# Two casts to a slot on ScalarE, the head's exponential behind them, and the DMAs that move along

## The chip, the cores and the metric

The kernel runs on one core of a Trainium2 chip. It has five instruction streams: TensorE (PE, matmuls; PEld is its weight load), VectorE (DVE), ScalarE (ACT), GpSimd (POOL) and SyncE (SP), which issues nearly all DMAs here. [...] The metric is the device time of one execution in microseconds, with the median of several runs. All inputs are float32, one sequence of 2048 tokens with width 512.

## What is computed

Four residual layers, of two kinds in turn (A, B, A, B). With 32 heads of width 16:

```python
def _A_ref(x, wqkv, w_phi, wo):      # linear attention over softmax features
    ...
    phi_q = jnp.concatenate([_softmax(pq, axis=-1), _softmax(-pq, axis=-1)], axis=-1)
    ...
def _B_ref(x, wq, wk, wv, wo, beta): # N = 4 segments of L = 512 tokens
    phi = lambda t: jnp.where(t > 0, t + 1.0, jnp.exp(t))
    ...
    for s in range(N):
        qs, ks, vs = q[:, :, s], k[:, :, s], v[:, :, s]
        logits = jnp.einsum("bhqd,bhkd->bhqk", qs, ks) * scale + mask
        p = _softmax(logits, axis=-1)
        a_dot = jnp.einsum("bhqk,bhkd->bhqd", p, vs)
        pq = phi(qs)
        num = jnp.einsum("bhld,bhde->bhle", pq, M)
        den = jnp.einsum("bhld,bhd->bhl", pq, z)[..., None] + 1e-6
        o = g * (num / den) + (1.0 - g) * a_dot
        pk = phi(ks)
        M = M + jnp.einsum("bhld,bhle->bhde", pk, vs)
        z = z + jnp.einsum("bhld->bhd", pk)
    ...
x = x + _A_ref(_layernorm(x), ...); x = x + _B_ref(_layernorm(x), ...)
x = x + _A_ref(_layernorm(x), ...); x = x + _B_ref(_layernorm(x), ...)
```

The change concerns the two B layers alone: causal softmax attention inside a segment of 512 tokens, plus a memory M, z that is read and written from segment to segment.

## The kernel before

**Half chunks and slots.** A B layer is one long hand-written order (`LayerB.steps`). Each of its 4 segments has 8 half chunks of 4 heads each, which I call h0 to h7. A half chunk is cut into R = 5 slots; the first is its *head* (slot 0), and slots 1 to 4 follow. In each slot `attend` puts score matmuls of the half chunk into the PSUM tile `lg`, of which there is one (`PS("lg", 1, ...)`), and ACT takes the exponential into `P`. So the `lg` matmuls of a slot wait for the exponential of the slot before. POOL zeroes the masked part of `P` (affine_select). Beside them `maxima` computes score maxima for a later half chunk (matmuls into `mx`, `my` or two `g` tiles, reduced by DVE into `mxs`), and the rest of a slot is filled with six steps of some projection.

**The head.** Slot 0 also does what a half chunk does once: transposes (`hh`, `oh`, `KN` and `mxs` rows: a matmul with `ident` into a `g` tile, which ACT then copies or casts out), memory reads and writes, and `weighted`, the 32 matmuls of `P` by `v` for the half chunk before. There are four `g` tiles (G = 4), so the matmuls of `weighted` wait until ACT has emptied a `g` tile of the head; ACT then moves their result into `U`.

**Projections in pairs.** `mm3_pair` runs two projections together on the two row halves of PE, in 24 steps, six in each of slots 1 to 4. The halves change places twice, before step 6 (the first of slot 2) and before step 18 (the first of slot 4). At each change PE waits for an empty instruction (`sync.nop`) on SP, which in turn waits for the matmuls of the step before. I call these two the first and the second handoff. They stand in SP's stream among its DMAs. Six steps of a pair are called Q (queries and keys of a chunk), V (values) or O (output projection) in the tables: h0 and h1 have Q2 and Q3, h2 and h3 O, h4 Q0 of the next segment, h5 V, h6 Q1, h7 V. In the last segment of a layer h2 to h5 have O (second B layer), or h2, h3 O and h4, h5 V of the next layer (first B layer).

**What follows a pair.** After a Q pair, at the end of slot 4, ACT copies the two results to `raw` (tiles `tb`), one for queries (m = 0) and one for keys (m = 1). `projected` then gives three jobs for each, which run some slots later (`self.at`): `parts` casts to `ta` (the high part; POOL subtracts the low part), `features` computes relu and exponential, `added` sums them on POOL. After an O pair ACT copies two results to `tb`, POOL adds them to the residual rows (`xr` or `mmq`), and SP stores these.

**Stacks.** `stack` has SP copy the high and low parts into the score operands (`e<-ta`, three DMAs for the queries, side 0, and three for the keys, side 1). It is called in the slots named by STACK for the half chunk three further on; the maxima of the next head read what it brings. A stack waits for `parts` where these were only just computed, which is so in h1, h5 and h7.

**Order.** Instructions of one engine keep the order in which the program names them (`Ordered`, `held`). In a slot this order is: scores and exponential, maxima, postponed jobs (`at`), stacks, the "<" entries of the table (head work), `weighted`, rows of the norm ("n", which run one slot after their entry), and last the six steps of the pair.

Of the kernel before, what the change touches and what calls it, by code (L numbers as in the profile page):

```python
# [10 lines left out]
AF = mybir.ActivationFunctionType  # L11
ALU = mybir.AluOpType
# [6 lines left out]
P = 128  # L19
NSEG = 4  # L20
# [12 lines left out]
G = 4  # L33
R = 5
TB3 = 5
STACK = (1, 3)
SPARE = (2, 4)
XR = 2
FILL = (1, 3, 4)
# [25 lines left out]
7.0 <max <a0+ | 7.1 fin V+/6 w      | 7.2 V+/6 n        | 7.3 V+/6 n | 7.4 V+/6 w  # L65
"""
GAPS = """
0.0 <max <a0 | 0.1 fin Q2/6 n       | 0.2 Q2/6 n        | 0.3 Q2/6 n cv3 | 0.4 Q2/6
1.0 <t0 <turn <max <a1 m0 | 1.1 fin Q3/6 | 1.2 Q3/6 n   | 1.3 Q3/6 | 1.4 Q3/6
2.0 <ln <t1 <turn <max <a1 m1 | 2.1 fin O/6 | 2.2 O/6   | 2.3 O/6 | 2.4 O/6  # L70
3.0 <ln <turn <turn <max <a2 | 3.1 fin O/6 | 3.2 O/6    | 3.3 O/6 | 3.4 O/6
4.0 <ln <ln <max <a2 | 4.1 fin Q0+/6 | 4.2 Q0+/6 cv0    | 4.3 Q0+/6 cv1 | 4.4 load begin Q0+/6
# [2 lines left out]
7.0 <max <a0+ | 7.1 fin V+/6      | 7.2 V+/6 n N        | 7.3 V+/6 n N | 7.4 V+/6  # L75
"""
LAST = """
0.0 <max <a0 | 0.1 fin Q2/6 n       | 0.2 Q2/6 n        | 0.3 Q2/6 n cv3 | 0.4 Q2/6
1.0 <turn <max <a1 | 1.1 fin Q3/6   | 1.2 Q3/6 n        | 1.3 Q3/6 | 1.4 Q3/6
2.0 <ln <turn <max <a1 | 2.1 fin O/6 | 2.2 O/6          | 2.3 O/6 | 2.4 O/6  # L80
3.0 <ln <turn <turn <max <a2 | 3.1 fin O/6 | 3.2 O/6    | 3.3 O/6 | 3.4 O/6
4.0 <ln <ln <max <a2 | 4.1 fin v/2  | 4.2 v/2 cv0       | 4.3 v/2 cv1 | 4.4 v/2
# [19 lines left out]
def interleave_kernel(ctx, tc, x_in, a_wqkv, a_wphi, a_wo, b_wq, b_wk, b_wv, b_wo, b_beta,  # L102
                      c_ident, c_mask, c_bd, out):
    nc = tc.nc
    MUL, ADD, SUB, MAX, MIN = ALU.mult, ALU.add, ALU.subtract, ALU.max, ALU.min
# [14 lines left out]
    def T2(tag, bufs, dt=F32, shape=(P, 512)):  # L120
        return sp.tile(list(shape), dt, tag=tag, bufs=bufs, name=nm(tag))

    def PS(tag, bufs, shape=(P, 512)):
        return ps.tile(list(shape), F32, tag=tag, bufs=bufs, name=nm(tag))
# [38 lines left out]
    dve, act, pool, sync = [Ordered(e) for e in (nc.vector, nc.scalar, nc.gpsimd, nc.sync)]  # L163
# [19 lines left out]
    def dma(out, in_):  # L183
        sync.dma_start(out=out.bitcast(F32), in_=in_.bitcast(F32))
# [319 lines left out]
    def out_pair(tiles, xdst, w, soon, w0=0, w1=D):  # L504

        pos = [PS("g", G) for _ in tiles]

        def side(po, o):
            return po[:, 0 : w1 - w0], o, lambda b, kc: w[b][:, kc, w0:w1]

        yield from mm3_pair(*[side(po, o) for po, (x, i, o) in zip(pos, tiles)])
        for po, (x, i, o) in zip(pos, tiles):
            y = T2("tb3", TB3)[:, 0 : w1 - w0]
            act.copy(y, po[:, 0 : w1 - w0])
            pool.tensor_tensor(out=x[:, w0:w1], in0=y, in1=x[:, w0:w1], op=ADD)
            if w1 == D:
                soon(lambda x=x, i=i: sync.dma_start(out=xdst[i], in_=x))
        yield

    def weigh(out, p, eps, add, eng=pool):  # L520
# [460 lines left out]
    class LayerB:  # L981
# [53 lines left out]
        def proj_pair(self, s, c):  # L1035

            self.st.setdefault((s, c), {})
            hT, ws = self.hT[s], self.w4
            pps = [PS("g", G) for _ in range(2)]

            def side(pp, w):
                return pp, lambda a, kc: w[:, a, kc, :], lambda b, kc: hT[b][:, kc, :]

            for n, _ in enumerate(mm3_pair(*[side(pp, w) for pp, w in zip(pps, ws)])):
                if n == 12:
                    for m in range(2):
                        self.queue_w(m, (0,))
                yield
            jobs = []
            for m in range(2):  # L1050
                self.queue_w(m, (1,))
                jobs.append(self.projected(s, c, m, pps[m]))
            for m, job in enumerate(jobs):
                for n, f in zip((1, 2, 3) if m == 0 else (2, 4, 5), job):
                    self.at.setdefault(self.k + n, []).append(f)
            yield

        def projected(self, s, c, m, pp):

            d = self.st[s, c]  # L1060
            hi, lo = d["part", m] = [T2("ta1", TA, F32R) for _ in range(2)]
            raw = T2("tb3", TB3)
            act.copy(raw, pp)

            def parts():
                act.copy(hi, raw)
                (pool if self.k >= R else dve).tensor_tensor(out=lo, in0=raw, in1=hi.bitcast(F32), op=SUB)
            todo = [parts]
            if not (s == 0 if m == 0 else s == NSEG - 1):
                e = d["phi", m] = T2("tb2", TB2)  # L1070

                def features():
                    act.activation(e, raw, AF.Relu, scale=-1.0)
                    act.activation(e, e, AF.Exp, scale=-1.0)
                    if m == 1:
                        act.activation(raw, raw, AF.Relu)

                def added():
                    if m == 0:
                        pool.tensor_scalar(raw, raw, 0.0, None, op0=MAX)  # L1080
                    pool.tensor_tensor(out=e, in0=raw, in1=e, op=ADD)
                todo += [features, added]
            return todo

        def sums(self, s, c):
# [107 lines left out]
        def attend(self, m):  # L1193


            s, c, hf = m // 8, m % 8 // 2, m % 2
            Q, K = [t[:, 2 * hf : 2 * hf + 2, :] for t in self.st[s, c]["set"]]
            self.pr[m] = {}

            def prod(pb, r, kb, at, w):  # L1200
                for e in range(2):
                    q, k = Q[64 * e : 64 * e + 64, r, :], K[64 * e : 64 * e + 64, r, :]
                    mm(pb[e][:, at : at + w], lhsT=k[:, kb * P : (kb + 1) * P],
                       rhs=q[:, 512 - w : 512], start=True, stop=True, tile_position=(64 * e, 0))

            for kbs, r in (((0,), 0), ((0,), 1), ((1, 3), 0), ((1, 3), 1), ((2,), None)):
                apart = self.thin and self.k > 8 * R * NSEG - 9 and self.k % 2
                if apart:
                    pb = [PS(t, 1) for t in ("mx", "my")]
                else:  # L1210
                    both = PS("lg", 1, (P, 2, 512))
                    pb = [both[:, e] for e in range(2)]
                pr = T2("P4", NP4, shape=(P, 2, 512))
                pq = pr.rearrange("p e (b x) -> p e b x", b=4)
                if kbs == (0,):
                    prod(pb, r, 0, 0, 512)
                    diags = [pr[:, :, 0:P]]
                elif kbs == (1, 3):
                    prod(pb, r, 3, 256, 256)
                    prod(pb, r, 1, 0, 384)  # L1220
                    diags = [pq[:, e, 0:4:3, :] for e in range(2)]
                else:
                    for rr in range(2):
                        prod(pb, rr, 2, 256 * rr, 256)
                    diags = [pr.rearrange("p e (r x) -> p (e r) x", r=2)[:, :, 0:P]]
                self.pr[m][kbs, r] = pr
                with tc.high_priority():
                    for out, src in ([(pr[:, e], pb[e]) for e in range(2)] if apart else [(pr, both)]):
                        act.activation(out, src, AF.Exp, scale=0.25)
                for diag in diags:  # L1230
                    pool.affine_select(out=diag, in_=diag, pattern=[[0, diag.shape[1]], [1, P]],
                                            compare_op=ALU.is_ge, fill=0.0, base=0, channel_multiplier=-1)
                yield

        def weighted(self, m):
# [75 lines left out]
        def out(self, s):  # L1311
            layer, i = (self.layer, NT - 4) if s < 0 else (self, 4 * s)
            for t in (0, 2):
                tiles = [(x, i + t + n, oT) for n, (oT, x) in enumerate(self.turned[0:2])]
                del self.turned[0:2]
                parts = 2 if self.thin and s == NSEG - 2 else 1
                for n in range(parts):
                    yield from out_pair(tiles, layer.xdst, layer.wo, lambda f: self.at.setdefault(self.k + (5 if s < NSEG - 2 else 2), []).append(f),
                                        n * D // parts, (n + 1) * D // parts)

        def early(self):
# [59 lines left out]
        def steps(self, side, after, table_end):  # L1381
# [3 lines left out]
            N = 8 * NSEG  # L1385
# [76 lines left out]
            for s in range(NSEG):  # L1462
                for cell in (FIRST if s == 0 else GAPS if s < NSEG - 1 else table_end).replace("|", "\n").split("\n"):
                    if cell.strip():
                        at_, *what = cell.split()
                        m, j = at_.split(".")
# [3 lines left out]
            for k in range(BEGIN, R * N + 1):  # L1470
                self.k = k
                if 0 <= k < R * N:
                    next(at)
                if MAXIMA <= k < MAXIMA + 2 * R or 2 * R - LEAD <= k < R * N - LEAD:
                    next(ma)
                put_off[0] = None
# [5 lines left out]
                m = k // R + 3  # L1482
                if 2 <= m < N:
                    for side_ in range(2):
                        if k % R == STACK[side_]:
                            self.stack(m, side_)
                what, s = table.get(k, ((), 0))
                for w in what:
                    if w[0] == "<":
                        do(w[1:], s, k)  # L1490
                if k % R == 0 and 0 <= k // R - 1 < N:
                    self.weighted(k // R - 1)
                for f in self.rows:
# [91 lines left out]
```

## Time and profile before

| | |
|---|---|
| median of 3 runs | 1368.67 us (1368.21 to 1370.08) |
| the profiled execution | 1368.75 us, span 1367.0 us |
| PE busy | 1290.1 us, 94% of the span |
| ACT busy | 840.8 us, 62% |
| DVE, POOL busy | 1038.3 us (76%), 752.6 us (55%) |
| chain that ended last | PE 62%, DVE 14%, ACT 13%, issue 4%, POOL 3%, DMA 3% |

The B layers lie at about 285 to 697 us and 953 to 1365 us of the span. A row of the waits names the waiting engine and tile, what it waited for, the sum in us, the number of waits and the longest. A row of the timeline gives the start, the duration, engine, line, operation, output and inputs, the count of instructions merged into the row, and in brackets the idle time before it with the one that ended it. SPq rows are DMA issues on SP; their duration is that of the issue, not of the transfer.

### The profile page before, as it was taken

How to read it: one execution, taken by the hardware profiler on the slowest of the kernel's cores; microseconds unless marked ns; L12 is line 12 of the kernel's file. 1: busy time of each engine (PE TensorE's matmuls, PEld its weight loads, DVE VectorE, ACT ScalarE, POOL GpSimd, SP SyncE). 2: the span in 40 equal slices, each digit the busy share in tenths (PEclk: the TensorE clock that was granted, in tenths of full speed). 3: DMA queues.
4: the chain of work that ended last, by engine and by line, in shares of the span. 5: the costliest groups of instructions: out<-in, count | busy, mean ns of one | idle time of the engine just before them, and what ended most of it. 6: DMA issues, size and time to landing. Idle time of an engine off the chain costs nothing.

```text
span 1367.0 us, 41870 instructions
## 1 busy us (share of the span) xinstructions
PE 1290.1 (94%) x16552; PEld 989.6 (72%) x16552; DVE 1038.3 (76%) x3247; ACT 840.8 (62%) x1274; POOL 752.6 (55%) x1116
## 2 busy tenths in 40 slices
PE   7999989999999999999899998999999999999987
PEld 6887868776766766777668886786776777677665
DVE  4766778787887887887757767787788788787884
ACT  5556345547787677676644334454677767767754
POOL 1568666225557667666334446551456566666653
PEclk9999999999999999999999999999999999999999
DMA  5398437544554444546341103745455454444432
GB/s 204 101 338 272 147 126 233 175 110 131 173 163 138 138 129 122 146 131 170 103 155 63 63 32 125 231 150 165 137 151 180 134 145 119 135 122 115 121 80 78
DMA packets 134419, 196.58 MB, mean 144 GB/s; under 512 B 15440, under 2 KB 61648, under 8 KB 133456
## 3 DMA queue, kind: packets, MB, share of 16 engines
q1 hardware_dynamic: 132256, 193.27, 46.7%
q8 instruction: 131, 2.15, 0.6%
q10 hardware_dynamic: 1968, 0.64, 0.2%
q14 instruction: 64, 0.52, 0.1%
HBM read 101.05 MB, written 39.85 MB: 103 GB/s over the span
## 4 chain that ended last, share of the span: by engine, by line
PE 62%; DVE 14%; ACT 13%; issue 4%; POOL 3%; DMA 3%; SPq 1%; ACTq 0%; DVEq 0%; POOLq 0%
PE g L177 48%; ACT P L155 6%; PE lg L177 5%; ACT tb L155 3%; PE g L181 3%; DVE g L155 3%; PE mx L177 3%; DVE U L155 2%; PE lg L181 2%; DVE mx L155 2%; DVE my L155 1%; ACT ta L155 1%; DVE es L155 1%; PE my L177 1%; DVE mxs L155 1%
## 5 line engine op out<-in xcount | busy, mean ns | idle before, releaser
L155 ACT ACTIVATE P<-lg 128x1024 f32<-128x1024 f32 x316 | 324.6, 1027 | 109.5 <-PE lg L177 89.1
L155 POOL TENSOR_SCALAR_AFFINE_SELECT P<-P 128x256 f32<-128x256 f32 (+1 forms) x448 | 190.7, 443 | 230.5 <-ACT P L155 217.7
L155 DVE CUSTOM_DVE_ANT_0 mx<-mx,mask 128x512 f32<-128x512 f32 (+2 forms) x316 | 158.6, 502 | 92.6 <-PE my L177 78.2
L155 DVE CUSTOM_DVE_ANT_0 g<-g,mask 128x128 f32<-128x128 f32 (+3 forms) x392 | 189.4, 539 | 10.9 <-PE g L177 10.9
L177 PE MATMUL g<-hh,wqk 64*128 64x512 f32 (+1 forms) x960 | 181.6, 393 | 1.6 <-SPq L155 1.3
L177 PE MATMUL lg<-e,e 64*128 64x512 f32 (+1 forms) x1010 | 147.2, 348 | 23.6 <-ACT P L155 22.3
L177 PE MATMUL g<-w,oh 64*128 64x512 f32 (+2 forms) x848 | 162.3, 382 | 2.6 <-ACT oh L155 2.6
L155 DVE CUSTOM_DVE_ANT_0 my<-my,mask 128x512 f32<-128x512 f32 (+2 forms) x316 | 164.1, 519 | 0.0
L177 PE MATMUL g<-P,v 128*32 128x128 f32 (+3 forms) x2064 | 151.6, 433 | 10.9 <-POOL xr L155 6.0
L177 PEld LDWEIGHTS lg<-e,e 64*128 64x128 f32 x1010 | 92.5, 185 | 78.9 <-ACT P L155 47.1
L177 PE MATMUL g<-w,hh 64*128 64x512 f32 (+1 forms) x672 | 142.9, 395 | 2.3 <-ACT w L155 1.3
L155 DVE DVE_READ_ACCUMULATOR2_ANT mxs<- 128x1 f32 x1024 | 144.6, 141 | 0.0
L177 PEld LDWEIGHTS g<-P,v 128*32 128x32 f32 x2064 | 65.2, 109 | 72.5 <-issue 54.9
L177 PEld LDWEIGHTS g<-hh,wqk 64*128 64x128 f32 (+1 forms) x960 | 97.4, 185 | 22.1 <-SPq L155 3.3
L177 PEld LDWEIGHTS g<-w,oh 64*128 64x128 f32 (+1 forms) x848 | 95.0, 188 | 19.9 <-ACT oh L155 3.5
L155 ACT ACTIVATE U<-g,share 128x512 f32<-128x512 f32 (+1 forms) x65 | 44.3, 682 | 101.2 <-PE g L177 101.1
L177 PE MATMUL g<-w,ol 64*128 64x512 f32 (+2 forms) x424 | 101.9, 379 | 0.1
L177 PE MATMUL g<-hl,wqk 64*128 64x512 f32 (+1 forms) x480 | 100.3, 389 | 0.0
L177 PEld LDWEIGHTS g<-w,hh 64*128 64x128 f32 (+1 forms) x672 | 83.0, 188 | 18.5 <-ACT w L155 1.6
L155 ACT COPY tb<-g 128x512 f32<-128x512 f32 (+1 forms) x132 | 70.9, 574 | 38.7 <-PE g L177 37.0
L155 POOL TENSOR_TENSOR ta<-tb,ta 128x512 fp32r<-128x512 f32 x56 | 72.2, 1289 | 35.9 <-ACT ta L155 33.2
L177 PE MATMUL g<-w,hl 64*128 64x512 f32 (+1 forms) x336 | 88.8, 393 | 0.0
(164 smaller groups left out, 2965.3 us busy)
## 6 DMA issues: line engine op xcount, KB each, us to landing
e<-ta SPq DMA_DIRECT2D x384, 128.0 KB
wqk<-wqk SPq DMA_DIRECT2D x128, 256.0 KB
x<-x SPq DMA_DIRECT2D x48, 256.0 KB
pq<-tb SPq DMA_DIRECT2D x24, 256.0 KB
tb<-pq SPq DMA_DIRECT2D x24, 256.0 KB
x<-xr SPq DMA_DIRECT2D x22, 256.0 KB
xr<-x SPq DMA_DIRECT2D x20, 256.0 KB
x<-in SPq DMA_DIRECT2D x16, 256.0 KB
```

The costliest lines, as they stand in the source:

```text
L155: i = f(*a, **k)
L177: return held(nc.tensor.matmul(*a, **k))
L181: return held(nc.tensor.transpose(*a))
```

## The change

Five edits, all in the B layers:

1. `parts` of the queries moves from the head to slot 1, beside the keys' `parts`; the features of the queries from slot 1 to slot 2. Of the keys' three feature activations the last becomes a job of its own (`clipped`), a slot later. `added` comes a slot later in both.
2. In a head, the exponential and its affine_select are put behind the postponed jobs and the "<" work, so behind the casts out of `g`. In slots 1 to 4 they stay where they were.
3. The residual additions on POOL come two slots after the copies of an O pair (in slot 1), and the stores four slots after them (slot 3), where before the additions came at once and the stores five slots later (slot 4), or two in the last segment.
4. STACK is (2, 3): the queries' stack is called in slot 2, not in slot 1.
5. One step of the norm moves from behind slot 1.2 to behind 0.0.

```diff
-STACK = (1, 3)
+STACK = (2, 3)
...
-0.0 <max <a0 | 0.1 fin Q2/6 n       | 0.2 Q2/6 n        | 0.3 Q2/6 n cv3 | 0.4 Q2/6
-1.0 <t0 <turn <max <a1 m0 | 1.1 fin Q3/6 | 1.2 Q3/6 n   | 1.3 Q3/6 | 1.4 Q3/6
+0.0 <max <a0 n | 0.1 fin Q2/6 n     | 0.2 Q2/6 n        | 0.3 Q2/6 n cv3 | 0.4 Q2/6
+1.0 <t0 <turn <max <a1 m0 | 1.1 fin Q3/6 | 1.2 Q3/6     | 1.3 Q3/6 | 1.4 Q3/6
...
             act.copy(y, po[:, 0 : w1 - w0])
-            pool.tensor_tensor(out=x[:, w0:w1], in0=y, in1=x[:, w0:w1], op=ADD)
+            soon(2, lambda x=x, y=y: pool.tensor_tensor(out=x[:, w0:w1], in0=y, in1=x[:, w0:w1], op=ADD))
             if w1 == D:
-                soon(lambda x=x, i=i: sync.dma_start(out=xdst[i], in_=x))
+                soon(4, lambda x=x, i=i: sync.dma_start(out=xdst[i], in_=x))
...
-                for n, f in zip((1, 2, 3) if m == 0 else (2, 4, 5), job):
+                for n, f in zip((2, 4, 5, 6) if m else (2, 3, 4), job):
...
-                    if m == 1:
-                        act.activation(raw, raw, AF.Relu)
+
+                def clipped():
+                    act.activation(raw, raw, AF.Relu)
...
-                todo += [features, added]
+                todo += [features] + [clipped] * m + [added]
...
-                    yield from out_pair(tiles, layer.xdst, layer.wo, lambda f: self.at.setdefault(self.k + (5 if s < NSEG - 2 else 2), []).append(f),
+                    yield from out_pair(tiles, layer.xdst, layer.wo, lambda late, f: self.at.setdefault(self.k + late, []).append(f),
...
                 if 0 <= k < R * N:
                     next(at)
+                    if k % R:
+                        self.weights()
...
                 for w in what:
                     if w[0] == "<":
                         do(w[1:], s, k)
+                if k % R == 0 and 0 <= k < R * N:
+                    self.weights()
```

**ACT, in h1 of the second segment of the second B layer** (from about 1070 us on in the profile before), first as it stood. `P<-lg` is an exponential, `ta` a cast of `parts`, `tb<-tb` a feature activation, `KN<-g` and `mt<-g` copies out of `g` tiles in the head, `U` the result of `weighted`:

```order
L155 ACTIVATE P_2806_16197<-lg_16196 128x1024
L155 CAST ta_2797_16185<-tb_2799_16187 128x512
L155 COPY KN_16220<-g_16215 128x512
L155 ACTIVATE mt_16226<-g_16224 16x128
L155 ACTIVATE U_16283<-g_16266,share 128x512
L155 ACTIVATE P_2822_16307<-lg_16306 128x1024
L155 DMA e_2257_13338<-mt_16226 2x8x128
L155 ACTIVATE tb_2800_16189<-tb_2799_16187 128x512
L155 ACTIVATE tb_2800_16189<-tb_2800_16189 128x512
L155 CAST ta_2801_16191<-tb_2803_16193 128x512
L155 ACTIVATE P_2831_16349<-lg_16348 128x1024
L155 ACTIVATE P_2835_16382<-lg_16381 128x1024
```

and now:

```order
L155 COPY KN_16217<-g_16212 128x512
L155 ACTIVATE mt_16223<-g_16221 16x128
L155 ACTIVATE P_2806_16198<-lg_16197 128x1024
L155 ACTIVATE U_16282<-g_16265,share 128x512
L155 ACTIVATE P_2822_16306<-lg_16305 128x1024
L155 DMA e_2257_13338<-mt_16223 2x8x128
L155 CAST ta_2797_16186<-tb_2799_16188 128x512
L155 CAST ta_2801_16192<-tb_2803_16194 128x512
L155 ACTIVATE P_2831_16345<-lg_16344 128x1024
L155 ACTIVATE tb_2800_16190<-tb_2799_16188 128x512
L155 ACTIVATE tb_2800_16190<-tb_2800_16190 128x512
L155 ACTIVATE P_2835_16381<-lg_16380 128x1024
```

The head's exponential moved behind `KN` and `mt`, and the queries' cast left the head. Slot 1 had three instructions behind its exponential and has two; slot 2 had none and has two.

**SP, in h4 of the same segment** (about 1115 to 1123 us before), first as it stood. The e_2257 rows are the queries' stack, the e_2258 rows the keys' stack, `wqk` the next weights, `out<-` the stores. The list has no row for a handoff; its wait for PE is printed with the row behind it, where PE_49 then stands first:

```order
L155 DMA e_2257_13338<-ta_2842_16450 32x2x512 [waits DMAHW2_49,PE_49]
L155 DMA e_2257_13338<-ta_2842_16450 32x2x512 [waits DMAHW3_49]
L155 DMA e_2257_13338<-ta_2843_16451 32x2x512 [waits DMAHW4_49]
L155 DMA e_2258_13339<-ta_2846_16456 32x2x512 [waits PE_49,DMAHW6_49]
L155 DMA e_2258_13339<-ta_2847_16457 32x2x512 [waits DMAHW7_49]
L155 DMA e_2258_13339<-ta_2846_16456 32x2x512 [waits DMAHW0_49]
L155 DMA wqk_12907<-wqk_80 128x2x256 [waits DMAHW1_49,PE_49]
L155 DMA wqk_12908<-wqk_81 128x2x256 [waits DMAHW2_49]
L155 DMA out<-mmq_16749 128x512 [waits PE_49,DMAHW3_49,Pool_49]
L155 DMA out<-xr_16751 128x512 [waits DMAHW4_49,Pool_49]
```

and now:

```order
L155 DMA e_2257_13338<-ta_2842_16449 32x2x512 [waits PE_49,DMAHW3_49]
L155 DMA e_2257_13338<-ta_2842_16449 32x2x512 [waits DMAHW4_49]
L155 DMA e_2257_13338<-ta_2843_16450 32x2x512 [waits DMAHW5_49]
L155 DMA out<-mmq_16745 128x512 [waits DMAHW6_49,Pool_49]
L155 DMA out<-xr_16747 128x512 [waits DMAHW7_49,Pool_49]
L155 DMA e_2258_13339<-ta_2846_16455 32x2x512 [waits DMAHW0_49]
L155 DMA e_2258_13339<-ta_2847_16456 32x2x512 [waits DMAHW1_49]
L155 DMA e_2258_13339<-ta_2846_16455 32x2x512 [waits DMAHW2_49]
L155 DMA wqk_12907<-wqk_80 128x2x256 [waits DMAHW3_49,PE_49]
L155 DMA wqk_12908<-wqk_81 128x2x256 [waits DMAHW4_49]
L155 DMA x_17178<-x_12_126 128x512 [waits PE_49,DMAHW5_49]
```

Before, the first handoff stood ahead of the keys' stack and the second ahead of the stores, with five DMAs between them. Now the first stands ahead of the queries' stack and the second behind `wqk`, with ten DMAs between them. The order of PE and of DVE is the same as before.

More of the change, by code (lines that the diff above doesn't have):

```diff
@@ L77 @@
 LAST = """
-0.0 <max <a0 | 0.1 fin Q2/6 n       | 0.2 Q2/6 n        | 0.3 Q2/6 n cv3 | 0.4 Q2/6
-1.0 <turn <max <a1 | 1.1 fin Q3/6   | 1.2 Q3/6 n        | 1.3 Q3/6 | 1.4 Q3/6
+0.0 <max <a0 n | 0.1 fin Q2/6 n     | 0.2 Q2/6 n        | 0.3 Q2/6 n cv3 | 0.4 Q2/6
+1.0 <turn <max <a1 | 1.1 fin Q3/6   | 1.2 Q3/6          | 1.3 Q3/6 | 1.4 Q3/6
 2.0 <ln <turn <max <a1 | 2.1 fin O/6 | 2.2 O/6          | 2.3 O/6 | 2.4 O/6
@@ L1226, in attend, with weights @@
                 self.pr[m][kbs, r] = pr
-                with tc.high_priority():
-                    for out, src in ([(pr[:, e], pb[e]) for e in range(2)] if apart else [(pr, both)]):
+                pairs = [(pr[:, e], pb[e]) for e in range(2)] if apart else [(pr, both)]
+                def weights(pairs=pairs, diags=diags):
+                    for out, src in pairs:
                         act.activation(out, src, AF.Exp, scale=0.25)
-                for diag in diags:
-                    pool.affine_select(out=diag, in_=diag, pattern=[[0, diag.shape[1]], [1, P]],
-                                            compare_op=ALU.is_ge, fill=0.0, base=0, channel_multiplier=-1)
+                    for diag in diags:
+                        pool.affine_select(out=diag, in_=diag, pattern=[[0, diag.shape[1]], [1, P]],
+                                           compare_op=ALU.is_ge, fill=0.0, base=0, channel_multiplier=-1)
+                self.weights = weights
                 yield
```

## The prediction

> **What bounds the kernel now.** I read the page first, then what PE waited for, then the timeline of one segment slot by slot.
>
> ```profile
> span 1367.0 us, 41870 instructions
> PE 1290.1 (94%) x16552; PEld 989.6 (72%) x16552; DVE 1038.3 (76%) x3247; ACT 840.8 (62%) x1274; POOL 752.6 (55%) x1116
> ...
> 300.00:690.00 390.00, 368.79 (x5428) 274.04 (x5429) 308.32 (x1167) 279.95 (x417) 233.22 (x385) 1.00 0.49 140
> 970.00:1290.00 320.00, 305.37 (x4510) 228.57 (x4504) 256.38 (x982) 234.03 (x351) 200.10 (x324) 1.00 0.49 138
> ```
>
> PE is the bound. In these two windows (length, then busy time of PE, PEld, DVE, ACT, POOL), which hold nearly all of the B layers, it is idle for 21 and 15 us. PE's order does not change, so the change can give only what PE waits for, and costs only what new waits it makes.
>
> ```profile
> PE lg L177 <- ACT P L155: 22.3, 56, 2.1
> PE g L181 <- DVE mxs L155: 9.9, 14, 1.3
> PE g L177 <- POOL xr L155: 6.0, 7, 0.9
> ...
> PE g L177 <- ACT mt L155: 2.9, 4, 0.7
> ...
> PE g L177 <- ACT KN L155: 2.0, 2, 1.0
> PE g L177 <- SPq L155: 1.5, 6, 0.4
> ```
>
> The first row is the score tile waiting for the exponential. The rows of `xr`, `mt` and `KN` are all `weighted` in a head. The last is the one to remember: PE waiting at a handoff for SP.
>
> **Term 1, slots 1 to 4: ACT's load evened out.** The ends of two half chunks, by the starts of their score matmuls: first h3, where ACT has no features, then h1, where it has.
>
> ```profile
> 1105.76 0.45 PE L177 MATMUL lg<-e,e 64*128 64x256 f32 x4
> 1107.70 0.40 PE L177 MATMUL lg<-e,e 64*128 64x256 f32 x4
> 1108.18 0.63 PE L177 MATMUL g<-w,oh 64*128 64x512 f32 x4
> 1109.58 0.40 PE L177 MATMUL lg<-e,e 64*128 64x512 f32 x2
> ...
> 1079.72 0.40 PE L177 MATMUL lg<-e,e 64*128 64x256 f32 x4
> 1080.59 0.50 PE L177 MATMUL g<-hh,wqk 64*128 64x512 f32 x2 [0.24 <-SPq L155]
> 1082.78 0.49 PE L177 MATMUL lg<-e,e 64*128 64x512 f32 x2 [0.53 <-DMA wqk<-wqk]
> ```
>
> Unhindered, slots 3 and 4 take 1.94 and 1.88 us. Slot 4 of h1 takes 3.06, though only 0.77 us of idle time is recorded, because matmul ends are modelled: slot lengths are the better measure. Over both layers up to 1289 us, 74 slots are longer than that, by 33.6 us in all, from the one that ends here
>
> ```profile
> 311.38 0.49 PE L177 MATMUL lg<-e,e 64*128 64x512 f32 x2 [0.26 <-DMA wqk<-wqk]
> ...
> 1285.80 0.39 PE L177 MATMUL lg<-e,e 64*128 64x256 f32 x2 [0.29 <-ACT P L155]
> ...
> 634.00:637.50 3.50, 3.50 (x22) 2.81 (x20) 1.98 (x9) 1.55 (x2) 3.42 (x5) 0.52 0.35 85
> ```
>
> to the one that ends in the second row. From this go 1.7 us of the granted clock at 0.52 in the window above, and about 1 us of handoffs: 31 us are ACT's. The cause, in slot 3 of h1:
>
> ```profile
> 1078.38 1.03 ACT L155 ACTIVATE P<-lg 128x1024 f32<-128x1024 f32 x1 [0.72 <-PE lg L177]
> 1079.30 1.81 ACT L155 ACTIVATE tb<-tb 128x512 f32<-128x512 f32 x3
> 1081.01 0.80 ACT L155 ACTIVATE x<-x,st 128x512 f32<-128x512 f32 x1
> 1081.72 1.00 ACT L155 ACTIVATE P<-lg 128x1024 f32<-128x1024 f32 x1
> ```
>
> From exponential to exponential are 3.34 us, in a slot of 1.94. Now two activations (0.92 + two thirds of 1.71, so 2.06 us) stand in slots 2 and 3, two casts in slot 1, and the norm's `x` is gone from there. An overrun of 0.1 us a slot is left, which the 0.3 us between an exponential's end and the next scores nearly hide: I leave 0.2 us for each of h2 and h5 and 0.6 for the h7 that also has the norm's root, 4 us in all. **Gain 27 us** (bounds: 16, if the recorded idle time were the truth, the 22.3 without the last stretch's 6, which one `lg` tile alone causes; and 31).
>
> **Term 2, heads: the casts ahead of the exponential.**
>
> ```profile
> 1110.73 1.04 ACT L155 ACTIVATE P<-lg 128x1024 f32<-128x1024 f32 x1
> 1111.65 1.09 ACT L155 CAST hh<-g 128x512 fp32r<-128x512 f32 x2
> 1112.59 0.26 ACT L155 ACTIVATE mt<-g 16x128 fp32r<-16x128 f32 x1
> 1113.00 2.36 PE L177 MATMUL g<-P,v 128*32 128x512 f32 x32 [0.90 <-POOL xr L155]
> 1115.29 0.50 PE L177 MATMUL lg<-e,e 64*128 64x512 f32 x2
> ```
>
> `weighted` starts 0.15 us after ACT's `mt` ends (1112.85) and frees a `g` tile; `xr` ended too, but it is not an operand. With the exponential behind, `mt` ends 0.92 us sooner, and this wait of 0.90 is gone. The exponential then ends at about 1113 us, before slot 1 asks for `lg` at 1115.29. The thirteen such waits are 0.8 us on average: **gain 11 us** (6.0 + 2.9 + 2.0; bounds 5 to 11). POOL's select of the head comes later too; only the next head reads it, five slots on.
>
> **Term 3, SP: the price.** A handoff is in order with SP's DMAs, and PE cannot pass it:
>
> ```profile
> 556.80 2.68 SPq L155 DMA_DIRECT2D wqk<-wqk  x2
> ...
> 558.71 0.43 PE L177 MATMUL g<-e,e 63*128 63x512 f32 x2
> 559.59 0.49 PE L177 MATMUL g<-hh,wqk 64*128 64x512 f32 x2 [0.45 <-SPq L155]
> ```
>
> Here the two issues ahead of the second handoff took 2.68 us by chance (1.07 below), SP came free at 559.48, and PE's step 18 began 0.11 us later. That is 0.64 later than usual, where it follows 0.24 behind the maxima's matmul (1108.18 is 0.48 behind its scores). So SP's lateness is paid in full. And SP's room is known:
>
> ```profile
> 1104.11 1.81 SPq L155 DMA_DIRECT2D e<-ta  x3
> 1108.04 0.34 SPq L155 DMA_DIRECT2D out<-xr  x1
> 1108.47 0.38 SPq L155 DMA_DIRECT2D out<-mmq  x1
> 1108.95 1.82 SPq L155 DMA_DIRECT2D e<-ta  x3
> ...
> 1117.52 1.81 SPq L155 DMA_DIRECT2D e<-ta  x3
> 1119.43 1.07 SPq L155 DMA_DIRECT2D wqk<-wqk  x2
> ```
>
> The keys' stack begins at the first handoff (1104.11), the stores at the second (1108.04); PE takes step 18 at 1108.18, so there are 4.07 us. The queries' stack of h4 ran early, at 1108.95, ahead of the first handoff. Now both stacks stand in that gap, each 1.91 us to the next issue: 3.82. With `wqk` (1.07) and 0.12 to PE, less 4.07, PE is late by 0.94 us in h0 and h6, and as much in h1, where the stacks also wait for `parts`: the casts come sooner, and POOL's subtractions end when they did. Two stores (0.9) move in at h3, late by 0.75, and at h4 with `wqk`, by 1.9; they wait for POOL's second addition, which ends about then. h2, h5 and h7 have two stacks alone, and just fit. That is 5.5 us a segment, 33 for six; the last segments, with fewer stacks but shorter slots, about 8, and two weight loads in h7 of both first segments 1: **42 us**. Such issues are sometimes long:
>
> ```profile
> 1063.96 1.25 SPq L155 DMA_DIRECT2D e<-ta  x1
> ```
>
> If every fifth of some 36 tight chains has one like it, 0.65 us over the median of 0.6, that is 5 us more. **Cost 47 us** (bounds: 0, if the handoff were not held; 60, with a long issue in every second chain and more stores late).
>
> [...]
>
> **Term 4, DVE.** The late handoff of h6 gives DVE time, and DVE was what the next head waited for:
>
> ```profile
> 1150.48 0.28 PE L181 MATMUL g<-ident,mxs 128*16 128x128 f32 x1 [0.95 <-DVE mxs L155]
> ```
>
> Five of the 14 waits on `mxs` are of this kind: **gain 5 us** (bounds 0 and 9.9). The rest of the change costs nothing that PE sees: `added` and the additions run on POOL (55% busy) with several slots in hand, and the keys' stack still lands before the next head's maxima, since it now holds that head back itself.
>
> **Sum.** -27 - 11 + 47 - 5 = +4 us on 1368.75 (span 1367.0 and 1.75 around it), which is the median of the runs to within 0.1 us: **1373 us**. It is a small difference of two large terms.
>
> **Rivals.** (a) *SP does not hold PE*: the handoff passes among the issues, or the queries' stack runs where it ran. Then only the gains are left, 1368.75 - 38 (terms 1 and 2; term 4 needs the lateness) = 1331 us. For it: only 1.5 us are recorded on this wait. Against it: 559.59 and 1080.59. [...] (b) *The two balance, or ACT gains a little more*: term 3 without long issues and h1 free, 1360 to 1371 us. (c) *ACT's evening fails*: exponential and two activations are 2.06 us in a slot of 1.94; should that add up rather than hide, half of term 1 is lost, and SP costs what it costs: 1386 us. (d) *Landing*: stacks so late that the next head's maxima wait for their data too, half a microsecond in 30 half chunks, 1388 us. Against it: the head is late by the same amount.
>
> **Chances.** Forecast 0.45, (a) 0.07, (b) 0.35, (c) 0.08, (d) 0.05. Less than 0.2% (2.7 us) is about what a measurement of this kernel can't tell from none. Of the forecast's and (b)'s share some 0.22 falls within 0.2%; faster by more is the rest of (b) and (a), 0.28; slower by more 0.50. The range of 1357 to 1387 us leaves out (a) and part of (c) and (d); the forecast alone has 1367 to 1382.
>
> **What would show it.** In the profile after, PE's waits on P at `lg` should fall from 22.3 to about 10, those of `weighted` on xr, mt and KN from 10.9 to near 0, and PE's waits on SPq should rise from 1.5 to 20 or more, at step 18 of h0, h1, h3, h4 and h6, with the longest in h4 near 1.5 us. Slots 2 and 3 of h1 should be below 2.0 us. If SPq stays below 5 us, the third term is wrong and the kernel is clearly faster; if P at `lg` stays above 15, the first is.

## The result, and the profile after

| | before | after |
|---|---|---|
| median | 1368.44 us (1367.16 to 1370.08), 4 runs | 1416.15 us (1413.45 to 1424.45), 4 runs |
| the profiled execution, its span | 1368.75 us, 1367.0 us | 1413.45 us, 1411.7 us |
| mean granted clock of PE | 0.996 | 0.987 |

The ratio is 1.0358 (95%: 1.0312 to 1.0404): slower by 3.6%, on the side the prediction held likelier, but 43 us above its number and 29 above its range. The page and PE's waits of the changed kernel, for the lines shown of before:

```profile
span 1411.7 us, 41898 instructions
PE 1305.8 (92%) x16552; PEld 994.7 (70%) x16552; DVE 1045.1 (74%) x3247; ACT 844.6 (60%) x1274; POOL 757.0 (54%) x1116
...
PE g L177 <- SPq L155: 52.3, 45, 3.8
PE lg L177 <- ACT P L155: 8.6, 21, 1.3
...
PE mx L177 <- DMA e<-ta: 5.0, 5, 1.6
...
PE g L181 <- DVE mxs L155: 3.6, 5, 0.9
...
PE g L177 <- ACT mt L155: 0.8, 5, 0.2
PE g L177 <- ACT KN L155: 0.5, 2, 0.3
```

The score tile's wait fell from 22.3 to 8.6 us, `xr` has no row any more, `mt` and `KN` nearly none, `mxs` lost 6 us. All that came as forecast. The first row is where the time went: 1.5 us before, 52.3 now, against "20 or more", and its longest wait is 3.8 us, where 1.5 was forecast. PE is also 15.7 us longer *busy* with the same 16552 matmuls, which no term of the prediction foresaw.

**Where it lies in a half chunk.** By the starts of the score matmuls, 58 half chunks of before can be set beside their counterparts of after. The sum of their differences: heads -1.4 us, slot 1 -0.1, slots 2 and 3 -14.3, slot 4 +53.5. The first and last half chunks of the layers and the A layers make up the other 7 of the 44.7 us between the two profiled executions. So ACT's evening shows in slots 2 and 3, and slot 4, whose projection steps begin with the second handoff, takes back more than three times as much. SP and PE in h4 of the second segment of the second B layer, the place shown in the section on the change:

```profile
1148.53 1.82 SPq L155 DMA_DIRECT2D e<-ta  x3
1150.45 0.53 SPq L155 DMA_DIRECT2D out<-mmq  x1
1151.17 0.34 SPq L155 DMA_DIRECT2D out<-xr  x1
1151.57 1.82 SPq L155 DMA_DIRECT2D e<-ta  x3
1153.48 1.08 SPq L155 DMA_DIRECT2D wqk<-wqk  x2
...
1154.67 0.50 PE L177 MATMUL g<-hh,wqk 64*128 64x512 f32 x2 [1.96 <-SPq L155]
```

Ten DMAs stand between the handoffs. The first starts 0.3 us after the scores of slot 2, the last ends at 1154.56, and PE's step 18 starts 0.11 us later: the picture of term 3. But slot 4 then takes 4.59 us, 2.73 more than its 1.86, while PE waited only 1.96. Most of the rest is in the clock. Two windows of 3.41 us (length, then busy time of PE, PEld, DVE, ACT, POOL, then the granted clock):

```profile
1152.15:1155.56 3.41, 1.45 (x16) 1.00 (x14) 3.33 (x13) 2.15 (x3) 3.41 (x7) 1.00 0.93 263
1155.56:1158.97 3.41, 3.41 (x19) 2.33 (x15) 1.09 (x7) 1.12 (x3) 0.80 (x1) 0.50 0.89 258
```

Behind a window in which PE was busy for 1.45 us stands one at half clock, where two matmuls of 64x512 take 0.63 us instead of 0.40. Six such windows stand behind h4's handoffs, three in each B layer; before has none there. By the mean clock (1 less the clock, times the span), 18.4 us of work time are withheld in this execution (1.3% of 1411.7) and 5.5 in that of before (0.4% of 1367.0).

### The profile page after: what moved, and what is told of

It reads as the page before. It is cut to its first block, busy times and chain, and to the rows that moved or that the text cites. A ratio compares the mean times of both kernels' runs of the same rounds, so it can differ in the third digit from the quotient of the medians.

```text
span 1411.7 us, 41898 instructions
## 1 busy us (share of the span) xinstructions
PE 1305.8 (92%) x16552; PEld 994.7 (70%) x16552; DVE 1045.1 (74%) x3247; ACT 844.6 (60%) x1274; POOL 757.0 (54%) x1116
## 4 chain that ended last, share of the span: by engine, by line
PE 65%; DVE 9%; SPq 6%; POOL 6%; ACT 5%; issue 5%; DMA 3%; ACTq 0%; DVEq 0%; POOLq 0%
PE g L177 51%; SPq L155 6%; PE lg L177 4%; PE g L181 4%; PE mx L177 3%; POOL P L155 2%; ACT P L155 2%; PE lg L181 2%; DVE g L155 2%; DMA e<-ta 1%; POOL ta L155 1%; DVE es L155 1%; PE my L177 1%; POOL xr L155 1%; ACT U L155 1%
## 5 line engine op out<-in xcount | busy, mean ns | idle before, releaser
L177 PE MATMUL g<-hh,wqk 64*128 64x512 f32 (+1 forms) x960 | 185.7, 402 | 34.9 <-SPq L155 34.8
L177 PEld LDWEIGHTS g<-w,oh 64*128 64x128 f32 (+1 forms) x848 | 94.3, 188 | 35.0 <-SPq L155 15.7
L177 PE MATMUL mx<-e,e 63*128 63x256 f32 (+3 forms) x323 | 85.5, 329 | 7.4 <-DMA e<-ta 5.0
```

The lines of the kernel that those rows point to most:

```text
L177: return held(nc.tensor.matmul(*a, **k))
```

## The experiments

The theory: SP's issues, in order between the handoffs, make the time, and long waits of PE add half-clock windows. Rivals: ACT's new order costs it (A), or the stacks' transfers do (L). All ratios are to the kernel before on the same chip (medians 1369.0 to 1370.1 us).

**1. The queries' stack back in slot 1**, all else as changed.

```diff
-STACK = (2, 3)
+STACK = (1, 3)
```

> The changed kernel with the queries' stack called in slot 1 again, all else as changed. Theory (SP's issues in order between the handoffs make the time): between the handoffs stand at most the keys' stack, two stores and two weight loads, 3.9 us of issues in a room of 4.07, so the second handoff is no longer late, and the six half-clock windows behind h4 go, since no wait there is long. But in h1, h5 and h7 the queries' stack now waits in slot 1 for the parts cast in the same slot, and the first handoff stands behind it: about 1 to 1.6 us each, some 20 times. PE's waits for SPq 20 to 35 us, at step 6 and not at step 18; time 1350 to 1372 us. Rival A (the new places of ACT's work or of the head's exponential cost the time, SP's lateness only shows it): these stay, so 1400 us or more. Rival L (transfers: the stacks land too late or collide): the same six DMAs in a half chunk, 1.9 us earlier for half of them; 1395 to 1410 us.

Measured: 1423.57 us, ratio 1.0395 (1.0371 to 1.0419), slower than the changed kernel. The theory in its simple form, that only the count of issues matters, failed, and the time lies where rival A had it (1400 or more); experiments 2, 4 and 9 decide about A. Two things hold PE. First, the expected wait for parts, in h1, h5 and h7, where slot 2 is 32 us longer in sum than before:

```profile
1112.01 3.95 SPq L155 DMA_DIRECT2D e<-ta  x6
...
1114.00 0.50 PE L177 MATMUL g<-hh,wqk 64*128 64x512 f32 x2 [1.44 <-SPq L155]
```

The queries' stack can only start at 1112.01, its third issue ends near 1113.9, and the first handoff comes behind it. Second, and not expected, slot 4 of h3 and h4 stayed 10.7 and 26.2 us longer than before, although only the keys' stack, two stores and, in h4, two weight loads stand between the handoffs:

```profile
1140.72 0.34 SPq L155 DMA_DIRECT2D out<-xr  x1
1142.16 0.34 SPq L155 DMA_DIRECT2D out<-mmq  x1
1142.59 3.81 SPq L155 DMA_DIRECT2D e<-ta  x6
```

Between the two stores SP stands still for 1.1 us: the second waits for something. Experiment 6 takes this up. The half-clock windows, which were expected to go, became more: 14 in the B layers, with a mean clock of 0.980 in this execution.

**2. The stack's new place alone**, in the kernel before: `STACK = (2, 3)` and nothing else.

> The kernel before with the queries' stack in slot 2 and nothing else changed; ACT's and POOL's order as before, stores behind the second handoff. Theory: h0, h4 and h6 have 3.82 + 1.07 us of issues in a room of 4.07, some 22 waits of 0.9 to 1.3 us at the second handoff, and h1 to h3, h5 and h7 little; no wait reaches 1.9 us, so no more half-clock windows than before. PE's waits for SPq 18 to 30 us; time 1385 to 1395 us. Rival A (ACT's new order is what costs): 1366 to 1372 us, SPq below 5. Rival L (transfers): PE waits for e<-ta at the maxima, not for SPq; 1375 to 1385 us.

Measured: 1407.47 us, 1.0272 (1.0249 to 1.0296); PE's waits for SPq 35.8 us in 35 waits, for `e<-ta` 2.0. Rivals A and L fall: ACT's order is that of before, the landings hardly count, and the price is there. It is above the range I gave. A clean chain, h4 of the second segment again:

```profile
1147.13 3.75 SPq L155 DMA_DIRECT2D e<-ta  x6
1150.97 1.07 SPq L155 DMA_DIRECT2D wqk<-wqk  x2
...
1152.15 0.50 PE L177 MATMUL g<-hh,wqk 64*128 64x512 f32 x2 [0.84 <-SPq L155]
```

Step 18 is due 0.48 us behind the scores of slot 4, which start at 1150.69, so at 1151.17; it starts at 1152.15, 0.98 late (0.94 by the prediction), and slot 4 as a whole is 1.10 longer. The mean of slot 4 over its 1.86 us is more: 1.47 in h0, 1.27 in h6 and 2.03 in h4, since in many chains one issue is a long one, 0.37, 0.11 and 0.72 us of these means. Against the expectation, two half-clock windows stand behind h4 (at 572.6 and 1043.7 us).

**3. The stores back behind the second handoff**, all else as changed (five slots after the copies; in last segments four).

```diff
-    lambda late, f: self.at.setdefault(self.k + late, []).append(f),
+    lambda late, f: self.at.setdefault(self.k + (late if late == 2 else 5 if s < NSEG - 2 else 4), []).append(f),
```

> The changed kernel with the stores of an O pair five slots after the copies again (so behind the second handoff; in the last segment still four), the additions and all else as changed. Theory: 0.9 to 1.3 us of issues leave the room of h3 and h4. h3 is then nearly free (it costs 9.7 us over 8 half chunks now), h4 is late by about 1 us instead of 2 to 3, and with no wait of 1.9 us the six half-clock windows are gone: 20 to 30 us less than the changed kernel, 1386 to 1396 us, SPq 22 to 35. If the half-clock windows do not hang on the length of that wait, only the issues are gained: 1400 us. Rival A (ACT's order): 1410 to 1418 us.

Measured: 1399.78 us, 1.0225 (1.0193 to 1.0256), 16 us less than the changed kernel, where 20 to 30 were expected. As expected, slot 4 of h3 (8 half chunks) went from 9.7 to 2.7 us over before, that of h4 from 23.3 to 15.3, and of the six half-clock windows behind h4 one is left, in a last segment, behind a wait of 4.6 us. Two new ones, at 1352.0 us, follow the last segment's h4 of the second layer, where PE waited 0.95 us for SP and 1.41 for the stack's data. But waits for SP remain (42.7 us), and they cover what ACT has gained: slot 4 of h1 is 0.5 us longer than before, where ACT's edits alone (experiment 9) make it 0.5 shorter.

**4. ACT's part without SP's.** The changed kernel with the queries' stack in slot 1, their parts in the head as before, and the stores of experiment 3.

```diff
-STACK = (2, 3)
+STACK = (1, 3)
...
-                for n, f in zip((2, 4, 5, 6) if m else (2, 3, 4), job):
+                for n, f in zip((2, 4, 5, 6) if m else (1, 3, 4), job):
```

> The changed kernel without what SP was given: the queries' stack in slot 1, the queries' parts in the head as before (their features still in slot 2), stores five slots after the copies. Left of the change are the keys' features dealt to two slots, the queries' features a slot later, the head's exponential behind the casts, the later additions and the norm's step. Theory: gains of terms 1 and 2 without the price, so 1332 to 1345 us; SPq below 4 us, P at lg 6 to 12, weighted's waits on xr, mt and KN below 3, clock windows as before. Rival A: 1365 us or more.

Measured: 1352.26 us, 0.9872 (0.9847 to 0.9896). So ACT's edits do gain, and rival A is refuted; but 7 us of the expectation were missing. One wait for SP of 3.04 us, in h4 of a last segment, and a half-clock window right behind it explain 5 of them. Left of the edits on POOL and SP were the later additions and, in the last segments, the later stores, which the next runs separate.

**5. The head's exponential alone** (edit 2) in the kernel before.

```diff
                 if 0 <= k < R * N:
                     next(at)
+                    if k % R:
+                        self.weights()
...
+                if k % R == 0 and 0 <= k < R * N:
+                    self.weights()
```

> The kernel before with the head's exponential and its affine_select behind the head's copies and nothing else changed. The prediction's term 2: the thirteen waits of weighted go and the heads shorten by their length, 11 us, so 1357 to 1360 us, and POOL xr, ACT mt and ACT KN together fall from 10.9 to below 1 us. Rival (the head is as long as before, because what weighted gains is given back at the next scores, which now wait for the later exponential, or at mxs): the heads of the ACT part alone were only 2.6 us shorter in sum; by that 1365 to 1369 us, with the waits on P at lg or on mxs larger by what the others lost.

Measured: 1364.01 us, 0.9949 (0.9929 to 0.9970): 5 us by the medians, 7 by the ratio (4 to 10 by its interval), a smaller gain than expected (1357 to 1360 us). In the profiled execution the heads are 8.6 us shorter. The copies now run straight behind one another, and the exponential behind them:

```profile
1106.97 1.08 ACT L155 CAST hh<-g 128x512 fp32r<-128x512 f32 x2
1107.93 0.26 ACT L155 ACTIVATE mt<-g 16x128 fp32r<-16x128 f32 x1
1108.10 1.00 ACT L155 ACTIVATE P<-lg 128x1024 f32<-128x1024 f32 x1
...
PE lg L177 <- ACT P L155: 21.7, 54, 1.6
```

The head of h4 takes 5.00 us where it took 5.71, 0.7 of its 0.9 us of wait. The waits on `xr`, `mt` and `KN` fall from 10.9 to 3.2 us (below 1 was expected), and the next scores do not wait in exchange (21.7 against 22.3), so the rival is out. Term 2 holds within its bounds, in their lower part.

**6. The residual sums alone** (edit 3) in the kernel before.

```diff
-            pool.tensor_tensor(out=x[:, w0:w1], in0=y, in1=x[:, w0:w1], op=ADD)
+            soon(2, lambda x=x, y=y: pool.tensor_tensor(out=x[:, w0:w1], in0=y, in1=x[:, w0:w1], op=ADD))
...
-                soon(lambda x=x, i=i: sync.dma_start(out=xdst[i], in_=x))
+                soon(4, lambda x=x, i=i: sync.dma_start(out=xdst[i], in_=x))
```

> The kernel before with the residual additions two slots after the copies and the stores four slots after (edit 3), nothing else changed: queries' stack in slot 1. Theory after the first runs: the addition that ends last decides, not the count of issues. The additions start behind slot 2's affine_select and take 2.8 us on POOL; the second store waits for them, the keys' stack (1.9 us) stands behind it, and so does the second handoff: h3 late by 1.3 us, h4, with the weight loads, by 2 to 3, some of them followed by a half-clock window. 10 + 16 to 26 us, so 1395 to 1407 us, SPq 22 to 35. Rival (the count of issues alone, as the prediction had it): 1.9 + 0.9 + 1.1 us fit into 4.07, so 1368 to 1375 us, SPq below 6.

Measured: 1409.55 us, 1.0284 (1.0259 to 1.0310), 2.5 us above the range: as expensive as the stack's move, though between the handoffs stand only seven DMAs at most. POOL, SP and PE in h4:

```profile
1147.25 1.30 POOL L155 TENSOR_TENSOR mmq<-tb,mmq 128x512 f32<-128x512 f32 x1
1148.51 1.48 POOL L155 TENSOR_TENSOR xr<-tb,xr 128x512 f32<-128x512 f32 x1
1148.58 0.34 SPq L155 DMA_DIRECT2D out<-mmq  x1
...
1150.01 0.34 SPq L155 DMA_DIRECT2D out<-xr  x1
1150.39 1.81 SPq L155 DMA_DIRECT2D e<-ta  x3
...
1152.32 1.19 SPq L155 DMA_DIRECT2D wqk<-wqk  x2
...
1153.62 0.50 PE L177 MATMUL g<-hh,wqk 64*128 64x512 f32 x2 [2.06 <-SPq L155]
```

Each store goes 0.02 to 0.03 us behind its addition, and the keys' stack, which has nothing to do with either, goes behind the stores. Slot 4 is 1.5 us longer on average in h3 and 2.8 in h4, and seven half-clock windows follow these handoffs, five of them behind h4. This also explains experiment 1: there, too, the second store waited for its addition.

**7 and 8. Nothing but issues.** The kernel before with six, or twelve, further stores of 32 KB to scratch memory in slot 2 of each h3.

```diff
+                if k % R == 2 and 0 <= k and k // R % 8 == 3:
+                    for j in range(12):
+                        sync.dma_start(out=scrap[j], in_=mask[:, 0:64])
```

> The kernel before with twelve further small stores (128 rows of 256 bytes from a constant tile to scratch memory that nobody reads) issued in slot 2 of each h3, between the two handoffs, ahead of the keys' stack. No data of the program moves through them. Theory: SP needs 0.40 to 0.43 us for each, 5 us in all, of which 1.75 are slack in h3: the second handoff is late by 3.2 to 3.5 us in 8 half chunks, 26 to 28 us. A wait of that length leaves PE busy for less than half of one 3.41 us window of the clock, so a window at half clock follows each, 1.7 us more: 38 to 42 us in all, 1406 to 1412 us, 8 half-clock windows more than before. If waits of PE do not lower the clock: 1394 to 1398 us. Rival (what holds PE is the stacks' transfers or their landing, not the issue of just any DMA): below 1376 us.

Measured with twelve: 1415.81 us, 1.0332 (1.0304 to 1.0360), 4 us above the range, and seven of the eight handoffs in h3 are followed by windows at half clock, three of them by two. SP and PE in one h3, and the clock behind another:

```profile
1133.42 6.51 SPq L155 DMA_DIRECT2D scrap<-mask  x12
1140.03 1.81 SPq L155 DMA_DIRECT2D e<-ta  x3
...
1141.95 0.80 PE L177 MATMUL g<-w,oh 64*128 64x512 f32 x2 [4.24 <-SPq L155]
...
1028.92:1032.33 3.41, 0.00 (x0) 0.00 (x0) 0.24 (x2) 0.00 (x0) 0.41 (x1) 1.00 0.35 78
1032.33:1035.74 3.41, 3.31 (x16) 2.65 (x18) 0.00 (x0) 0.35 (x1) 0.00 (x0) 0.50 0.94 265
```

> The kernel before with six, in place of twelve, of the small stores to scratch memory in slot 2 of each h3. From the run with twelve: 0.475 us from one to the next, so 2.85 us, of which 1.75 are slack; the second handoff is late by 1.1 us in 8 half chunks, 9 us, and one or two issues of over 1 us among these chains add 1 to 2 us. No wait is long enough to bring PE below half of a 3.41 us window, so no window at half clock is added: 1376 to 1382 us, SPq 9 to 14 us, and twice this price in issues plus the clock makes the 47 us of the twelve. If the clock falls behind waits of 1.1 us too: 14 us more, 1390 us or above. Rival (the twelve cost what they did by their transfers): 24 us, half of the twelve's price, 1392 us.

Measured with six: 1381.95 us, 1.0096 (1.0068 to 1.0124), and no half-clock window more than before in the B layers. PE's waits for SP are 8.0 us longer than before with six stores (9.5) and 30.6 with twelve (32.1); the time is 13 and 47 us longer. The 16 us that the twelve cost beyond the waits are the clock's: 22.6 us are withheld in that execution (1.6% of 1411.2), against 5.5 with six (0.4% of 1380.0) and before. (That the waits grow nearly fourfold with twice the stores is the slack of 1.75 us, which counts once; "twice this price" left that out.) No data of the program moves through these stores, so SP's time for issuing is enough to hold PE, and rival L is out. The window with the least work of PE in the B layers of the run with six, and the one behind it:

```profile
1117.76:1121.17 3.41, 1.72 (x14) 1.23 (x14) 1.02 (x4) 0.49 (x2) 0.64 (x1) 1.00 0.70 176
1121.17:1124.58 3.41, 2.77 (x83) 2.08 (x85) 2.54 (x10) 3.05 (x6) 2.77 (x3) 1.00 0.81 218
```

**9. ACT's edits alone.** The kernel before with edits 1, 2 and 5, but the queries' parts left in the head; additions, stores and stacks are those of before.

```diff
-                for n, f in zip((1, 2, 3) if m == 0 else (2, 4, 5), job):
+                for n, f in zip((2, 4, 5, 6) if m else (1, 3, 4), job):
...
-                    if m == 1:
-                        act.activation(raw, raw, AF.Relu)
+
+                def clipped():
+                    act.activation(raw, raw, AF.Relu)
...
-                todo += [features, added]
+                todo += [features] + [clipped] * m + [added]
```

> The kernel before with ACT's edits alone (the keys' features in two slots, the queries' features a slot later with their parts left in the head, the head's exponential behind the copies, the norm's step); residual additions, stores and both stacks as before. It differs from the ACT part run before in the residual additions and in the stores of the last segments. Theory: that run lost 3 us at one handoff (h4 of the last segment, at 651 us, the later addition ahead of the stack) and 1.7 us of clock behind it; without these 1345 to 1350 us, SPq below 3.5 us. Rival (the later additions help by easing POOL or ACT): 1352 us or more.

Measured: 1342.65 us (1340.76 to 1344.82), 0.9799 (0.9776 to 0.9821). It beats both kernels, and by more than I expected: without the later additions, and with the last segments' stores where they were, the run is 9.6 us faster than experiment 4 (on another chip; by the ratios, 10).

```profile
PE lg L177 <- ACT P L155: 9.9, 25, 1.3
PE g L181 <- DVE mxs L155: 7.8, 11, 0.9
...
PE g L177 <- SPq L155: 3.1, 6, 1.4
...
PE g L177 <- ACT mt L155: 2.2, 9, 0.4
...
span 1340.9 us, 41944 instructions
PE 1281.4 (96%) x16552; PEld 993.4 (74%) x16552; DVE 1040.6 (78%) x3247; ACT 843.0 (63%) x1274; POOL 753.0 (56%) x1116
```

The waits for SP stay small, and no half-clock window lies in the B layers.

**The sum of the parts.** ACT's edits alone -26.5 us (9), the stack alone +37.4 (2), the residual sums alone +40.5 (6): together +51.4, and the whole change has +47.7. So the loss lies in two edits that change SP's stream, either of which alone undoes ACT's gain. That the sum comes so near is partly chance, for the parts do not act independently. The kernel of experiment 3 has +29.7, where (9) and (2) make +10.9: 12 us of this difference lie in slot 4, where PE waits for SP in either case and ACT's gain is lost. The stores between the handoffs, in turn, cost 16 us beside the stack (experiment 3) and not 40. The move of the queries' `parts` to slot 1 is in none of the three and was not run alone.

## Why the prediction was wrong

**The mechanism was right**: SP in order between the handoffs, paid in full by PE. So was the sign, but by little merit: +4 us was a small difference of two large terms. The chances leaned to slower, but 28% stood on faster and 22% on the same, because the sum was read as two large terms in balance. They do not balance: 27 us of gain stand against some 74 of price (the changed kernel against run 9).

**Term 1 (-27 us)** was right in kind. Slots 2 and 3 are clean (1.96 and 1.93 us in h1, 1.94 and 1.90 in h5), and in run 9 slots 1 to 4 of the 58 half chunks are 19.6 us shorter: within the bounds of 16 to 31, but below the value taken.

**Term 2 (-11 us)** is 5 by the medians of run 5, within the bounds; its wait of 0.9 us in h4 yielded 0.7.

**Term 4 (-5 us)** came as worked out: the heads of h7 are 5.3 us shorter in the changed kernel and 0.6 in run 9, where h6 isn't late. Terms 2 and 4 together should have shortened the heads by 16 us, and they are 1.4 shorter. What is known of what took it back: waits of the maxima for the stacks' data, which are rival (d) in small (`DMA e<-ta`, 5.0 us in 5 waits, none in the rows of before's largest), and the half-clock windows, most of which reach into the heads of h5 (+3.5 us).

**Term 3 (+47 us, bounds 0 to 60) is the step that failed, by its size.** Against run 9, slot 4 of the 58 half chunks of the changed kernel is 62 us longer in sum, and their heads 7. How much slot 4 is longer than 1.86 us, mean of each half chunk of the changed kernel:

| | h0 | h1 | h2 | h3 | h4 | h5 | h6 | h7 |
|---|---|---|---|---|---|---|---|---|
| worked out, without long issues | 0.94 | 0.94 | 0 | 0.75 | 1.9 | 0 | 0.94 | 0 |
| measured | 1.34 | 1.11 | 0.56 | 1.20 | 3.02 | 0.25 | 1.24 | 0.66 |
| of it, long issues in the chain | 0.24 | 0.06 | 0.69 | 0.25 | 0.45 | 0.22 | 0.12 | 0.16 |

That is 9.4 us a segment for 5.5. (A long issue counts with what it has above 0.6 us, and part of it may fall into slack: h2.) Three things make the difference:
- *Long issues.* I took one in every fifth of 36 chains, 5 us. The profile of before had the rate: 23 of its 384 `e<-ta` issues took over 0.8 us. At one in seventeen, six such issues meet a long one in about every third chain. In the changed kernel 23 of some 60 chains have one, some 16 us in all. While the chains had slack, these cost little: in before PE waits for SP for 1.5 us in all.
- *The rest of a chain.* PE's step 18 follows the last issue by 0.11 us wherever SP held it, as I had taken (in 44 of 45 cases), and without long issues it is 0.94 to 1.00 us late in h0, by the prediction 0.94. But slot 4 is longer than step 18 is late by another 0.12 us, and two ordinary stores in h3 and h4 take 1.06 to 1.20 us to the next DMA, where I had 0.9. "h2, h5 and h7 just fit" left no room for any of this.
- *h4.* Ten DMAs without a long issue hold PE for 1.9 us and make slot 4 2.2 us longer, or 2.7 where the slow clock begins within it (1.9 worked out); with a long issue PE waits for 2.3 to 3.8 us (1.2 in one case). The clock falls behind six of the eight, with a long issue or without. The half-clock windows are in no term: these six and one near the end of the first B layer (at 701.6 us), 1.7 us each, 12 us. I had one of them in a quoted row of before (0.52 at 634 us), took it for a stray, and did not ask what stood ahead of it (PE busy for 1.30 us of a window of 3.41).

The remark that the stores "wait for POOL's second addition, which ends about then" was the other warning that I did not price. In the changed kernel the queries' stack ahead of the stores hides most of that wait; run 6 shows that it would have cost the same without the stack.

**The rivals.** (a), at 1331 us, is refuted by runs 2, 7 and 8: in run 8 each further DMA is 32 KB, and its 0.475 us in SP's queue is what PE waits for. (b) supposed no long issues. (c) did not occur: the score tile's waits fell by 13.7 us. (d) is real, but 5 us instead of 15.

## What to carry to other kernels

An engine that only issues DMAs can be a bound without any transfer of the program being late (in run 8 PE waits for SP for 30.6 us more, and the stores that make it wait are read by nobody): list what stands in its queue between two of its synchronisations, add up the issues, and keep slack for the long ones, whose rate can be counted in the trace (23 of 384 stack issues above 0.8 us in before). A DMA that waited for data put its wait on what stood behind it in that queue (in run 6 a store stood 1.1 us for its addition, and the keys' stack behind it), so it belongs behind what is urgent and not ahead of it. When an edit moves work on several engines, make each engine's part alone: here a gain of 2% was inside a loss of 3.6%.

## What the runs showed of the hardware

**The windows at half clock follow windows with little work of PE.** In the changed kernel the clock's records have the half-clock stretches of the B layers at 3.413 us each, and they begin on a grid of that step: those behind h4 lie 32, 95, 202, 234 and 266 steps behind the first. In the eleven traces of this case I laid that grid over the part from 285 to 1330 us, some 3300 windows at full clock. All 41 in which the records have PE busy for 1.58 us or less (46%) are followed by a window at half clock; of the others, 5 are. Two pairs of the changed kernel, on either side, and two neighbouring windows of the run with twelve stores:

```profile
462.66:466.07 3.41, 1.53 (x14) 1.27 (x16) 2.69 (x11) 1.52 (x2) 3.41 (x5) 1.00 0.93 262
466.07:469.48 3.41, 3.41 (x81) 2.54 (x81) 1.64 (x8) 2.31 (x5) 0.17 (x1) 0.50 0.93 283
623.08:626.49 3.41, 1.67 (x14) 1.41 (x16) 2.00 (x7) 2.08 (x3) 1.89 (x2) 1.00 0.88 242
626.49:629.90 3.41, 3.41 (x103) 1.91 (x101) 2.34 (x11) 2.12 (x4) 0.41 (x1) 1.00 0.68 226
...
1247.37:1250.79 3.42, 1.72 (x18) 1.19 (x14) 3.15 (x14) 1.75 (x2) 1.70 (x4) 1.00 0.31 67
1250.79:1254.20 3.41, 1.82 (x14) 1.24 (x14) 0.00 (x0) 0.12 (x1) 0.00 (x0) 1.00 0.73 192
```

So a window with 1.9 us of idle time was followed by one at half clock (the first pair), and a wait of 3.3 us across two windows was not: it stands in the one h3 of the run with twelve that has no half-clock window behind it. The one half of a window that the expectations of runs 7 and 8 take as the bound is not sharp in these records: a window with 1.61 us of work in run 4 was followed by one at half clock, and one with 1.62 in run 6 was not. The spread of the changed kernel goes with it: its four runs have spans of 1411.7, 1412.8, 1416.0 and 1422.7 us at mean clocks of 0.987, 0.988, 0.984 and 0.981.

**The time of an issue did not follow the bytes.** Stores of 256 KB (`out<-xr`) mostly took 0.34 to 0.45 us on SP, and 0.53 as the first behind a stack; stores of 32 KB (`scrap<-mask`) took 0.43, the stacks' 128 KB 0.53 to 0.60. Single issues of 0.8 us and more, up to 2.3 (241 of the 4224 `e<-ta` in the eleven traces), come among stacks, stores and weight loads, without a period that I could find; their cause stays open.
